# A pre-norm attention block and GeGLU network on one core: residual rows preset in PSUM, a seventh joint pair of F tiles, more turning by DMA, last heads passed on in halves

## The chip, the cores and the metric

The kernel runs on one core of a Trainium2 chip. The metric is device time of one execution in microseconds (us): the median of three runs of the kernel before is 639.09 us (638.98 to 639.78). A measurement of this kernel can tell a change from none from about 0.2% on. The core has TensorE (PE, matrix products into PSUM), VectorE (DVE), ScalarE (ACT), GpSimd (POOL), which sees SBUF only, and SyncE (SP), which issues every DMA here.

## The reference

All in float32, S = 2048 tokens, D = 512, H = 32 heads of 16, window of 8 keys with step 2, F = 1792:

```
qkv = layernorm(x) @ wqkv                       # D -> 3 D
logits[s, w] = q[s] . k[s - 2 w] / 4, w = 0..7  # per head, masked where s - 2 w < 0
o = softmax(logits) @ v[s - 2 w]
h = x + o @ wo
n = layernorm(h)
out = h + (gelu(n @ w_gate) * (n @ w_up)) @ w_down
```

## The kernel before, in words

**Tiling.** The tokens are cut into four chunks c = 0..3 of 512 (rows j = 0..3 of 128). Chunks 0 and 2 hold the even tokens, 1 and 3 the odd ones, so that the step of 2 falls away. Every product is done three times with operands split into a high and a low part (hi x hi, hi x lo, lo x hi), so a 512-wide contraction for 512 columns takes 12 matmuls of 128x512. `split` makes the parts: a cast on ACT and a subtraction on DVE or POOL.

**Projections.** For chunks 1 to 3 q and k of two row tiles are computed together by `project_pair`, with 7 block products of 6 matmuls (42) where the plain way takes 48; the sums that this scheme needs are made by `sums` (of x) and `weight_sums`. `prep` takes x already transposed from DRAM (`xt`) and subtracts the mean, which `stats` computes and PE spreads over the partitions with four transposes.

**Attention(c).** For four groups b of 8 heads, `logits` (products and sums on DVE), `softmax` and `values` (a product on DVE, a tree of additions `pv` on DVE or POOL). The output `o` is transposed, either by PE (`transpose4`, read from PSUM) or by a DMA (`crossed`: an ACT copy that separates the 16-bit halves, a transposing DMA, an ACT copy that joins them, then `split` from SBUF). `CROSS_O` lists the groups b for which the DMA does it; for chunk 0 there were none.

**Tail(c).** `wo` products for the four row tiles (12 matmuls each) into a PSUM bank, `aux` for chunks 1 and 2. DVE adds the residual rows (L775) into `h`, `norm` follows on DVE and POOL, then a transpose to hT, by DMA for chunks 1 and 2 (`CROSS_H`).

**FFN(c).** For each of the 14 F tiles f: a gate and an up product (12 matmuls each), gelu on ACT, a product on DVE, `split_g`, and two steps later (`flush`) the down product, 12 matmuls into the four banks `acc`. `finish` adds h to each bank on DVE (L875) and sends the rows out.

**The last two chunks (`last_two`).** F tiles are taken in pairs for chunks 2 and 3 together (`joint`), 7 block products of 6 matmuls for gate and 7 for up, that is 84 where two chunks and two tiles take 96. The first F tile of `EARLY` pairs is run for chunk 2 alone before (`early_step`), with its first half kept for the joint part. With `PAIRS = 6` two F tiles were left that both chunks did by themselves: chunk 2 ahead of the joint part, chunk 3 behind it. The gate-times-up results for chunk 3 are kept and their down products come last (`rest`).

**Order.** Every operation goes into a list with its engine, a duration and its dependencies. `schedule` runs the list as in time, by rank, and so fixes the order on each engine; `SHIFTS` are nudges to the ranks of stretches of the list, `SWAPS` move single operations between DVE and POOL. On the chip each engine works through its own instructions strictly in that order.

Of the kernel before, what the change touches and what calls it, by code (L numbers as in the profile page):

```python
# [16 lines left out]
P = 128  # L17
D = 512
# [20 lines left out]
FROM, TO = 52, 18  # L39
# [5 lines left out]
PAIRS = 6  # L45
EARLY = 2
# [192 lines left out]
def tile_block(ctx: ExitStack, tc: tile.TileContext, x: bass.AP, xt: bass.AP, wqkv: bass.AP, wo: bass.AP,  # L239
# [248 lines left out]
    def prep(c, j):  # L488
# [10 lines left out]
        if j % 2:  # L499
            sums(c, j // 2, xcs[j - 1], xc)  # L500
# [703 lines left out]
```

## Time and profile before

| | |
|---|---|
| median of three runs | 639.09 us |
| the profiled execution's own time | 640.41 us |
| its span, first to last instruction | 638.5 us |
| PE busy | 628.6 us (98%), 2816 matmuls and transposes |
| DVE, ACT, POOL busy | 497.4, 372.4, 386.9 us |
| DMA | 133.50 MB, mean 209 GB/s |
| granted TensorE clock | 0.999 |

A matmul's busy time is its own duration, and successive ones overlap, so a busy share of 98% tells where PE stood still but not how much work it had. The work is read from the start times: in a run of matmuls without waits one starts about every 0.227 us.

### The profile page before, as it was taken

Reading aid. Unit: us, or ns where it says so; the run is one execution under the profiler, and the core shown is the slowest. Engines: PE = TensorE matmul, PEld = TensorE weight load, DVE = VectorE, ACT = ScalarE, POOL = GpSimd, SP = SyncE. Lnnn points to the kernel's source line nnn. Section 1 sums busy time; section 2 is a strip of 40 time slices with the busy share of each in tenths; the row PEclk is TensorE's granted clock in tenths of the full one; section 3 lists DMA queues with packets and bytes.
Section 4 is the critical chain, followed back from the end, with each engine's and each line's share of the span. In section 5 each row is a group of like instructions: output and inputs, shape, how many; then the busy total and the mean of one; then the engine's idle time right before and its main releaser. Section 6 shows DMA issues by size and latency. Waiting matters only on the chain. (4 is left out here: it accounts for less than half of the span.)

```text
span 638.5 us, 8214 instructions
## 1 busy us (share of the span) xinstructions
PE 628.6 (98%) x2816; PEld 517.4 (81%) x2816; DVE 497.4 (78%) x548; ACT 372.4 (58%) x632; POOL 386.9 (61%) x350
## 2 busy tenths in 40 slices
PE   8999999999999999999999999999999999999997
PEld 8887788887888887877888788888888888888886
DVE  5879989999999999999989999978665633535322
ACT  6796444455554765776786579847455554533341
POOL 3598998943898798477647675628466876400000
PEclk9999999999999999999999999999999999999999
DMA  8759656497859969989997689960432123214362
GB/s 303 247 208 309 239 202 234 152 368 264 285 174 313 289 225 288 305 239 329 357 326 252 230 183 249 274 231 16 149 117 99 59 74 132 83 50 146 82 193 91
DMA packets 66857, 133.50 MB, mean 209 GB/s; under 512 B 24816, under 2 KB 24816, under 8 KB 66304
## 3 DMA queue, kind: packets, MB, share of 16 engines
q1 hardware_dynamic: 66816, 132.99, 63.7%
q8 instruction: 22, 0.36, 0.2%
q14 instruction: 19, 0.16, 0.1%
HBM read 101.19 MB, written 26.80 MB: 200 GB/s over the span
## 5 line engine op out<-in xcount | busy, mean ns | idle before, releaser
L740 POOL TENSOR_TENSOR pv<-pv 128x1024 f32<-128x1024 f32 (+1 forms) x51 | 99.6, 1964 | 20.6 <-DVE pv L735 19.8
L810 PE MATMUL acc<-dnh,gh 128*128 128x512 f32 x224 | 87.2, 390 | 0.0
L812 PE MATMUL acc<-dnh,gl 128*128 128x512 f32 x224 | 87.2, 389 | 0.0
L811 PE MATMUL acc<-dnl,gh 128*128 128x512 f32 x224 | 87.1, 389 | 0.0
L691 DVE TENSOR_TENSOR pk<-kw,qp 128x2048 f32<-128x2048 f32 x32 | 72.9, 2278 | 5.9 <-ACT qp L684 4.4
L735 DVE TENSOR_TENSOR pv<-vw,qp 128x2048 f32<-128x2048 f32 x32 | 72.4, 2279 | 1.7 <-ACT qp L684 0.5
L694 DVE TENSOR_REDUCE lg<-pk 128x128 f32<-128x2048 f32 x32 | 72.6, 2273 | 0.2
L399 PE MATMUL pg<-hTh,gu 128*128 128x512 f32 x256 | 68.9, 391 | 2.1 <-POOL gu L327 0.8
L399 PE MATMUL pu<-hTh,gu 128*128 128x512 f32 x256 | 68.7, 390 | 0.7 <-POOL gu L327 0.7
L399 PEld LDWEIGHTS pg<-hTh,gu 128*128 128x128 f32 x256 | 47.7, 188 | 13.3 <-ACT hTh L326 1.4
L399 PEld LDWEIGHTS pu<-hTh,gu 128*128 128x128 f32 x256 | 47.9, 188 | 11.0 <-POOL gu L327 1.2
L812 PEld LDWEIGHTS acc<-dnh,gl 128*128 128x128 f32 x224 | 42.0, 188 | 8.8
L810 PEld LDWEIGHTS acc<-dnh,gh 128*128 128x128 f32 x224 | 42.0, 188 | 8.8
L811 PEld LDWEIGHTS acc<-dnl,gh 128*128 128x128 f32 x224 | 42.0, 188 | 8.7
L327 POOL TENSOR_TENSOR gl<-g,gh 128x512 fp32r<-128x512 f32 x25 | 33.1, 1325 | 19.2 <-ACT gh L326 19.0
L327 POOL TENSOR_TENSOR gu<-fraw,gu 128x512 fp32r<-128x512 f32 x23 | 30.1, 1323 | 23.9 <-ACT gu L326 23.9
L326 ACT CAST gh<-g 128x512 fp32r<-128x512 f32 x44 | 27.2, 619 | 21.9 <-DVE g L867 12.0
L825 ACT CAST dnh<-fraw 128x512 fp32r<-128x512 f32 x40 | 24.6, 619 | 25.9 <-PE acc L812 17.3
L399 PE MATMUL pg<-hTl,gu 128*128 128x512 f32 x128 | 34.5, 391 | 0.4 <-DVE hTl L327 0.2
L399 PE MATMUL pu<-hTl,gu 128*128 128x512 f32 x128 | 34.2, 389 | 0.0
L1014 ACT COPY jt<-pa 128x512 f32<-128x512 f32 x32 | 18.8, 588 | 24.3 <-PE pa L982 20.0
L867 DVE TENSOR_TENSOR g<-pu,g 128x512 f32<-128x512 f32 x32 | 21.9, 684 | 11.3 <-PE pu L399 10.1
(290 smaller groups left out, 1509.3 us busy)
## 6 DMA issues: line engine op xcount, KB each, us to landing
fraw<-in_wffn_dram SPq DMA_DIRECT2D x46, 768.0 KB, 5.8
kw<-kv SPq DMA_DIRECT2D x16, 704.0 KB, 5.7
vw<-kv SPq DMA_DIRECT2D x16, 704.0 KB, 5.9
dnl<-ld SPq DMA_DIRECT2D x40, 256.0 KB, 3.0
gu<-ld SPq DMA_DIRECT2D x18, 512.0 KB, 4.5
kv<-qkvt SPq DMA_DIRECT2D x32, 256.0 KB, 2.6
ld<-gu SPq DMA_DIRECT2D x14, 512.0 KB, 4.4
x<-in_x_dram SPq DMA_DIRECT2D x16, 256.0 KB, 5.4
```

Of the source, the lines that this page charges most:

```text
L326: act(490 if psum_src else 525, lambda: nc.scalar.copy(hi(), src()), r, [wh])
L327: sub = lambda eng: eng.tensor_tensor(lo(), src(), hi().bitcast(F32), op=ALU.subtract)
L399: nc.tensor.matmul(acc(), a, b, start=(p == k == 0), stop=(p == n - 1 and k == KD - 1))
L691: nc.vector.tensor_tensor(pr(), k4, q2.unsqueeze(2).to_broadcast([P, 2, W, QF]), op=ALU.mult)
L694: dve(2195, lambda pr=pr, jj=jj: nc.vector.tensor_reduce(lg()[:, i, jj:jj + 2], pr().rearrange("p j w (h d) -> p j w h d", d=DH), axis=AX. ...
L735: nc.vector.tensor_tensor(pr().rearrange("p j w (h d) -> p j w h d", d=DH), v5, e5, op=ALU.mult)
L740: either(home, 256 * m, lambda eng, pr=pr, m=m: eng.tensor_tensor(pr()[:, :, 0:m], pr()[:, :, 0:m], pr()[:, :, m:2 * m], op=ALU.add), [], ...
L810: nc.tensor.matmul(a, gh()[:, sl], dh(), start=(i == 0), stop=False)
L811: nc.tensor.matmul(a, gh()[:, sl], dl(), start=False, stop=False)
L812: nc.tensor.matmul(a, gl()[:, sl], dh(), start=False, stop=(i == NF - 1))
L825: act(525, lambda: nc.scalar.copy(dh(), fr()[:, 2]), [(fr, None)], [(dh, None)])
L867: dve(605, lambda: nc.vector.tensor_tensor(g(), ps[1](), g(), op=ALU.mult), [(ps[1], None)], [(g, None)])
```

## The change

What it does, in parts:

1. **Preset PSUM.** `start(c)` copies the rows of h into the four `acc` banks, and the down products then all add to them (`start=False`); `finish` only copies a bank out (`evict`, on ACT, or on DVE by `SWAPS`). In `tail`, ten of the sixteen `wo` banks (`SEEDED`) are filled by ACT with the residual rows before the product; then the bank is copied to h on ACT and `bn_stats` reads the bank itself.
2. **Seventh pair** (`PAIRS` 6 to 7, `EARLY` 2 to 3): no F tile is left for a chunk alone. Chunk 2's down products of the early steps are all issued ahead of tail(3) (`DRAIN`); the ring for intermediate results in the joint part has 5 slots where it had 7 (`JT`).
3. **Turning by DMA** also for o of chunk 0, groups 0 to 2 (`CROSS_O`), and for x of chunk 3 (`CROSS_X`): the rows loaded for the statistics are centred by ACT, turned and split; `xt` is not read for it, and PE does not spread the mean.
4. **Halves.** The last group's o goes on in two parts of two row tiles (`HALVE`), and a `wo` product needs only its own part. Chunk 3's wo goes through three banks (`LASTB`), its residual rows into buffers of their own.
5. **Plain projection** of q and k for the first pair of chunk 1 (`PLAIN`): 48 matmuls, no `sums`.
6. The last row tile of the last chunk leaves PSUM in two halves, by ACT and DVE, with a DMA each; the order of the `qk` banks, the pace of attention (`TO` 18 to 22) and the tables `SHIFTS` and `SWAPS` are new.

```diff
-PAIRS = 6
-EARLY = 2
+PAIRS = 7
+EARLY = 3
-CROSS_O = ((), (0, 1, 2, 3), (0, 1, 2, 3), (0, 1, 2))
+CROSS_X = (3,)
+PLAIN = ((1, 0),)
+SEEDED = [(1, j) for j in (1, 2, 3)] + [(2, j) for j in range(4)] + [(3, j) for j in (1, 2, 3)]
+LASTB = ("qp", "mm0", "mm1", "qp")
+JT = ("q0", "q1", "o1", "lg", "ex")
+HALVE = (0, 1, 2, 3)
+CROSS_O = ((0, 1, 2), (0, 1, 2, 3), (0, 1, 2, 3), (0, 1, 2))
 SHIFTS = (
-    (232, 45, "PE", -8320), (1524, 9, "ACT", 7257), (1661, 68, "DVE POOL", 2376), (810, 7, "DVE", 146), (1093, 5, "DVE POOL", -8370),
+    (102, 130, "PE DVE ACT POOL SP", 1338), (1243, 51, "DVE POOL", 516), (1684, 47, "PE", 2945), (439, 11, "PE", -678), (1244, 116, "POOL", 483),
...
+    def evict(dst, src, r, w, home="ACT"):
+        ns = {"ACT": 490, "DVE": 605}
+        o = plan.add(home, ns[home], lambda: nc.scalar.copy(dst(), src()) if o.engine == "ACT" else nc.vector.tensor_copy(dst(), src()), r, w)
...
         if c in CROSS_X:
+            act(700, lambda: nc.scalar.activation(t(), t(), AF.Identity, bias=mv()[:, j, 0:1]), [(mv, j)], [(t, None)])
+            turn([(t, None)], t, xc)
...
+            if seeded:
+                act(490, lambda acc=acc, j=j: nc.scalar.copy(acc(), rows[j][0]()), rows[j][1], [(acc, None)])
             mm(acc, [...], "wo",
-               [[(oh, None), (wo_h, None)], [(oh, None), (wo_l, None)], [(ol, None), (wo_h, None)]])
-            dve(605, lambda hj=hj, acc=acc: nc.vector.tensor_tensor(hj(), acc(), hj(), op=ALU.add), [(acc, None), (h, None)], [(h, j)])
+               [rh + [(wo_h, None)], rh + [(wo_l, None)], rl + [(wo_h, None)]], seeded=seeded)
+            if seeded:
+                evict(hj, acc, [(acc, None)], [(h, j)])
+                xh = norm(hj, [(h, j)], f"h{c}_{j}", "ACT" if c in ONACT else "DVE", acc, [(acc, None)])
...
-            dve(605, lambda j=j: nc.vector.tensor_tensor(h()[:, j], accs[c][j](), h()[:, j], op=ALU.add),
-                [(accs[c][j], None)], [(h, j)])
+                evict(lambda j=j: h()[:, j], accs[c][j], [(accs[c][j], None)], [(h, j)], "DVE" if c == NC - 1 and j % 2 else "ACT")
     def start(c):
+        for j in range(J if SEED else 0):
+            evict(accs[c][j], lambda j=j: hres[c]()[:, j], [(hres[c], j)], [(accs[c][j], None)])
...
+        if DRAIN:
+            flush(c, 0)
         tail(d)
```

The tables also move instructions. Three places matter below. In the rows, the first name is what is written, then what is read; the last two numbers before the buffer's own are chunk and row (or F) tile, and what stands in brackets is the engine or DMA queue waited for.

On PE, at the end of chunk 2's FFN, the kernel before goes on like this (acc are the down products, pg and pu the gate and up products of chunk 3's own F tiles):

```order
L812 MATMUL acc_2_3_4180<-dnh_2_13_5134,gl_2_13_5326 128x512
L399 MATMUL pg_3_1_5362<-hTh_3_4034,gu_3_1_5142 128x512 x4
L399 MATMUL pg_3_1_5362<-hTl_3_4050,gu_3_1_5142 128x512 x4
...
L399 MATMUL pu_3_0_5421<-hTl_3_4050,gu_3_0_5288 128x512 x4
L399 MATMUL pu_3_0_5421<-hTh_3_4034,gu_3_0_5288 128x512 x4
L810 MATMUL acc_3_0_5436<-dnh_3_1_5222,gh_3_1_5413 128x512 [waits Activation_49]
```

and the changed kernel like this:

```order
L906 MATMUL acc_2_3_3916<-dnh_2_13_5254,gl_2_13_5441 128x512
L904 MATMUL acc_3_0_5476<-dnh_3_0_5340,gh_3_0_5419 128x512 [waits DVE_49]
L905 MATMUL acc_3_0_5476<-dnl_3_0_5338,gh_3_0_5419 128x512 [waits DMAHW3_49]
...
L904 MATMUL acc_3_1_5482<-dnh_3_0_5340,gh_3_0_5419 128x512 [waits Activation_49]
...
L904 MATMUL acc_3_2_5495<-dnh_3_0_5340,gh_3_0_5419 128x512 [waits Activation_49]
...
L904 MATMUL acc_3_3_5498<-dnh_3_0_5340,gh_3_0_5419 128x512 [waits Activation_49]
```

The 48 gate and up matmuls between the two chunks' down products are gone, and each bank's first down product of chunk 3 waits for the engine that presets it.

On ACT, at the same place, the changed kernel has these rows (h_2 from acc_2 is the copy out, acc_3 from h_3 the preset; rows 0 of the presets and 2 of the copies are on DVE):

```order
L349 CAST gh_3_1_5457<-gs_v1_4353 128x512 [waits PE_49,Activation_49]
L919 CAST dnh_3_2_5464<-fraw_3_2_5342 128x512 [waits DMAHW4_49,PE_49]
L308 COPY h_2_2828<-acc_2_0_3877 128x512 [waits PE_49]
L308 COPY h_2_2828<-acc_2_1_3927 128x512 [waits PE_49]
L308 COPY acc_3_1_5482<-h_3_4049 128x512 [waits Activation_49]
L308 COPY h_2_2828<-acc_2_3_3916 128x512 [waits PE_49]
L308 COPY acc_3_2_5495<-h_3_4049 128x512 [waits DVE_49]
L308 COPY acc_3_3_5498<-h_3_4049 128x512 [waits Activation_49]
```

None of these copies was there before; ACT had only casts at this place.

On ACT, in the tail of chunk 1, the changed kernel has these rows (wo_1 from h_1 is the preset, h_1 from wo_1 the copy out, a_o the copies around a transposing DMA):

```order
L860 COPY wo_1_1_2419<-h_1_1333 128x512 [waits DVE_49]
L349 CAST gh_0_11_2427<-g_0_11_2380 128x512 [waits DVE_49]
L377 COPY a_o_1_3_2_2396<-o_1_3_2283 128x2x256 [waits DMAHW1_49,Activation_49]
L349 CAST oTh_1_2024<-a_o_1_3_2_2396 128x256 [waits Activation_49]
L308 COPY h_1_1333<-wo_1_1_2419 128x512 [waits PE_49]
L860 COPY wo_1_2_2466<-h_1_1333 128x512 [waits DVE_49]
```

The copy out and the next preset stand behind a copy that waits for a transposing DMA; before, the bank was freed by one addition on DVE.

## Rows read from the trace of the kernel before

**Rows 1.** Stretches: length, busy of each engine (instructions), granted clock, DMA share, GB/s.

```profile
150.00:200.00 50.00, 49.79 (x221) 40.62 (x220) 47.50 (x39) 27.73 (x48) 38.82 (x28) 1.00 0.75 254
200.00:250.00 50.00, 48.48 (x213) 39.48 (x213) 49.46 (x41) 30.68 (x48) 43.10 (x33) 1.00 0.83 261
250.00:300.00 50.00, 48.49 (x212) 39.18 (x211) 45.41 (x51) 33.52 (x51) 30.66 (x28) 1.00 0.95 296
500.00:550.00 50.00, 50.00 (x222) 41.41 (x221) 21.46 (x27) 27.08 (x47) 37.13 (x40) 1.00 0.23 79
620.00:638.50 18.50, 14.58 (x65) 11.74 (x63) 4.97 (x8) 2.91 (x5) 0.00 (x0) 0.96 0.30 103
```

**Rows 2.** Chain that ended last: start, us from there to the next, what.

```profile
408.81 2.72 PE pg L399 x12
418.78 0.44 PE tp_o L338 x4
```

**Rows 3.** Waits of PE: who for whom, us in total, times, longest.

```profile
PE pg L399 <- POOL gu L327: 0.8, 1, 0.8
PE pg L399 <- ACT hTh L326: 0.8, 1, 0.8
PE pu L399 <- POOL gu L327: 0.7, 1, 0.7
PE pg L399 <- ACT g L861: 0.6, 1, 0.6
PE wo L399 <- DVE h L775: 0.5, 1, 0.5
```

**Rows 4.** Groups on DVE: busy, mean ns of one, idle before, releasers.

```profile
L775 DVE TENSOR_TENSOR h<-wo,h 128x512 f32<-128x512 f32 x16 | 11.0, 686 | 3.9 <-PE wo L399 3.8
L875 DVE TENSOR_TENSOR h<-acc,h 128x512 f32<-128x512 f32 x16 | 10.7, 687 | 7.0 <-PE acc L812 7.0
L602 DVE SCALAR_TENSOR_TENSOR qkvt<-qkb,mvx,qkvt 128x512 f32<-128x512 f32 x6 | 4.5, 743 | 1.5 <-PE qkb L585 1.5
L327 DVE TENSOR_TENSOR oTl<-tp_o,oTh 128x512 fp32r<-128x512 f32 x5 | 3.4, 686 | 1.0 <-ACT oTh L326 1.0
L327 DVE TENSOR_TENSOR oTl<-a_o,oTh 128x512 fp32r<-128x512 f32 x3 | 4.4, 1471 | 0.0
L327 DVE TENSOR_TENSOR hTl<-a_h,hTh 128x512 fp32r<-128x512 f32 x4 | 3.4, 856 | 0.5 <-ACT hTh L326 0.5
L740 DVE TENSOR_TENSOR pv<-pv 128x1024 f32<-128x1024 f32 x6 | 9.5, 1588 | 0.0
L740 DVE TENSOR_TENSOR pv<-pv 128x512 f32<-128x512 f32 x7 | 6.5, 930 | 0.1
L742 DVE TENSOR_TENSOR o<-pv 128x256 f32<-128x256 f32 x13 | 10.2, 794 | 0.0
```

**Rows 5.** Groups on ACT, columns as in rows 4.

```profile
L1014 ACT COPY jt<-pa 128x512 f32<-128x512 f32 x32 | 18.8, 588 | 24.3 <-PE pa L982 20.0 <-DVE pa L1020 4.3
L326 ACT CAST gh<-g 128x512 fp32r<-128x512 f32 x44 | 27.2, 619 | 21.9 <-DVE g L867 12.0 <-DVE g L1011 8.8 <-DVE g L1082 1.0
L350 ACT COPY a_o<-o 128x1024 uint16<-128x1024 uint16 x11 | 11.5, 1042 | 1.3 <-DVE o L742 1.1 <-DVE hTl L327 0.2
L354 ACT COPY a_o<-o 128x1024 uint16<-128x1024 uint16 x11 | 15.0, 1368 | 1.2 <-DMA o<-a_o 1.2
```

**Rows 6.** DMA issues: queue, form, count, KB each, median us to landing.

```profile
qd<-qkvt SPq DMA_DIRECT2D x12, 256.0 KB, 2.6
o<-a_o SPq DMA_TRANSPOSE x11, 4.3
```

**Rows 7.** Waits of ACT between 50 and 430 us, columns as in rows 3.

```profile
ACT dnh L825 <- DMA fraw<-in_wffn_dram: 6.1, 2, 4.2
```

**Rows 8.** Last instructions of PE and DVE in order of time: start, us, what.

```profile
633.51 0.39 PE L812 MATMUL acc<-dnh,gl 128*128 128x512 f32 x1
632.58 2.73 DVE L875 TENSOR_TENSOR h<-acc,h 128x512 f32<-128x512 f32 x4 [5.00 <-PE acc L812]
```

More of the change, by code (lines that the diff above doesn't have):

```diff
@@ L287, in either @@
         return o
+    def evict(dst, src, r, w, home="ACT"):
+        ns = {"ACT": 490, "DVE": 605}
+        away = "DVE" if home == "ACT" else "ACT"
+        o = plan.add(home, ns[home], lambda: nc.scalar.copy(dst(), src()) if o.engine == "ACT" else nc.vector.tensor_copy(dst(), src()), r, w)
+        o.other = away, ns[away]
+        return o
     def dma(dst, src, nbytes, r=(), w=(), eng=None, **k):
@@ L382, in norm, with mm @@
         return dst
-    def mm(acc, triples, nm, reads, chain=(), single=None):
+    def mm(acc, triples, nm, reads, chain=(), single=None, seeded=False):
         n = len(triples)
@@ L498, in prep @@
         xcs[j] = xc
-        if j % 2:
+        if j % 2 and (c, j // 2) not in PLAIN:
             sums(c, j // 2, xcs[j - 1], xc)
@@ L523, in sums @@
         plan.floor = 0
-    wT = {}
+    wT, held = {}, []
     def weight_sums():
@@ L543, in weight_sums, with put @@
             h, l, ph, pl = wT[i]
-            act(950, lambda h=h, src=src: nc.scalar.copy(h(), src()), [r], ph)
-            either("DVE", 1024, lambda eng, h=h, l=l, src=src: eng.tensor_tensor(l(), src(), h().bitcast(F32), op=ALU.subtract), [r] + ph, pl)
+            def put(h=h, l=l, ph=ph, pl=pl, src=src, r=r):
+                act(950, lambda: nc.scalar.copy(h(), src()), [r], ph)
+                either("DVE", 1024, lambda eng: eng.tensor_tensor(l(), src(), h().bitcast(F32), op=ALU.subtract), [r] + ph, pl)
+            if slot or not PLAIN:
+                put()
+            else:
+                held.append(put)
         for i, (s, h) in {0: (1, 0), 1: (1, 1), 6: (0, 1)}.items():
@@ L607, in project_pair @@
         product(0, A, True)
-        scaled(A, 1, j0)
-        product(1, B, True)
-        added(B, 1, j0)
+        if SEEDQK:
+            evict(B, A, [(A, None)], [(B, None)])
+            product(3, C, True)
+            product(1, B, False)
+            scaled(B, 1, j0)
+        else:
+            scaled(A, 1, j0)
+            product(1, B, True)
+            added(B, 1, j0)
         product(4, A, False)
         scaled(A, 0, j0)
-        product(3, C, True)
+        if not SEEDQK:
+            product(3, C, True)
         product(5, A, False)
@@ L1036, in joint @@
                 out_of((1, 1), C, u3, tmp[2 * n + s][-1])
-                if n == s == 0:
+                if n == s == 0 and not DRAIN:
                     flush(c, 0)
@@ L1140, in tile_block @@
             project_pair(c, p)
+            if held and (c, p) == PLAIN[-1]:
+                held.pop()()
         for j in range(J):
```

254 lines of the change are left out of this document (163 added, 91 removed), and 9 rows, old and new, of the table SWAPS.

## The prediction, made before the result was known

> **What bounds the kernel now.** I read the stretches first. PE is busy for 49.79 of 50 us at 150 to 200, for all 50 at 500 to 550, and falls short by 1.52 and 1.51 us in the two stretches from 200 to 300; at the end it has 14.58 of 18.5 [rows 1]. The granted clock is 1.00 in all but the last, so PE is at its upper level and no gain is to be had there. DVE is nearly full in the same front part (47.50, 49.46, 45.41 of 50) and half idle behind (21.46) [rows 1]. So behind about 360 us PE's own work is the time, and before that PE and DVE are close rivals. The chain of waits gives the price of PE's work: 12 matmuls of 512 columns in 2.72 us, 0.2267 each, and four transposes in 0.44, 0.11 each [rows 2]. The waits of PE after the start are few: 0.8, 0.8, 0.7, 0.6 and 0.5 us, 3.4 together; they fall at 238 to 288 us and at 359 and end with POOL, ACT and DVE [rows 3].
>
> **The change part by part.** The order of instructions gives the counts.
>
> *PE's work.* The seventh pair takes 84 matmuls where two plain steps took 96: 12 x 0.2267 = 2.72 us off. The plain projection of one pair adds 6: +1.36. Three groups of o of chunk 0 leave PE (12 transposes of 0.11, -1.32), and so does the spreading of chunk 3's mean (4, -0.44). Sum -3.12. All of it stands in PE's own queue, so it counts in full wherever PE is not waiting.
>
> *DVE up to the end of attention(3).* Of the additions of the residual to wo (686 ns), seven go in chunks 1 and 2 and one DVE copy, taken at the same price, comes: -4.1 us. Of the eight additions to acc (687 ns) in chunks 0 and 1 three stay as copies: -3.4. The plain pair drops three combined scalings (743 ns): -2.2. Chunk 0 drops four low parts of o from PSUM (686 ns) and gets two halves, which no row shows; I put one at 0.42, between half of 686 ns and all of it: -1.9. Four low parts of hT pass to POOL (856 ns): -3.4. Against that, `SWAPS` gives DVE four tree additions of 1024 (1588 ns) and five of 512 (930 ns) and takes six of the last step (794 ns): +6.4 + 4.7 - 4.8 = +6.3. Sum -8.7 [rows 4]. What it is worth is only the waits of PE which a lighter DVE, and a POOL relieved of those trees, can end: of the 3.4 us at most all, at least nothing. They ended with three engines, and one of these (ACT) gets heavier, so I take half: -1.7.
>
> Here a row speaks against the change: a low part of o read from PSUM takes DVE 686 ns, one read from SBUF after a DMA took 1471 [rows 4]. The Trainium skill (SBUF — State Buffer, Who interferes with whom) has the reason: a DVE instruction with two SBUF inputs waits while GpSimd reads SBUF, one with a single SBUF input does not. If all three turned groups of chunk 0 met POOL that way, DVE would have 3 x 0.785 = 2.4 us more, the relief would be 6.3 in place of 8.7, and my half would shrink to -1.2. The order puts most such low parts on POOL, so I keep -1.7.
>
> *Presets of the wo banks.* No row shows a copy from SBUF to PSUM. The nearest are ACT's copy out of PSUM, 588 ns, and its cast within SBUF, 619 [rows 5]; I take 0.6 for each preset and copy out, and the two are so close that the range does not need both. In chunk 1 the bank `aux` was freed by one DVE addition; now it needs a copy out (0.6, with `bn_stats` beside it on DVE) and the preset (0.6), some 1.5 us with the steps between them. Between the second wo product and the third the order leaves PE ten matmuls of other tiles, 2.27 us; between the third and fourth eight, 1.81. So the preset is hidden if ACT is free, with 0.3 to 0.8 to spare, and each microsecond that ACT is held longer is a microsecond of PE. Queued behind the waiting wo product on PE are FFN matmuls which nothing else delays. In chunk 2 eight lie between the first two products and thirty or more behind; chunk 3 has three banks. I take +0.5 for all ten, bounds 0 and +7 (see the slower rival).
>
> *Presets of acc.* For chunks 0 to 2 they come into banks that stand free before the first down product, behind several gate and up products, and cost nothing; without that cover it would be 0.7 per chunk. Between chunks 2 and 3 the cover is gone: the 48 gate and up matmuls that stood there are now joint work. From the end of the last product on acc_2_0 PE needs acc_3_0 after 3 x 0.68 = 2.04 us, and then one more bank every 0.68. ACT has first the cast of a g whose slot frees only one down product earlier, and a cast of down weights, so its first copy out starts about 0.6 late and ends at 1.2; DVE presets bank 0 by 2.0; ACT then copies bank 1, presets it by 2.45 (wanted at 2.72), copies bank 3 by 3.05 and presets bank 2 by 3.75, wanted at 3.40, and bank 3 by 4.3, in time. A stall of 0.35 with 0.6 per copy: +0.4, bounds 0 and +2 (the cast of weights waits for a DMA).
>
> *The last rows.* The last product on acc_3_2 starts at 633.51, three more follow, so PE ends at 633.51 + 3 x 0.227 + 0.39 = 634.58; DVE's four chained additions end at 632.58 + 2.73 = 635.31 [rows 8]. Two engines that share the four rows, with the last one halved, end about 0.45 behind PE, at 635.05. The transfers behind keep their length: -0.2, bounds -0.4 and +0.3 (two transfers of shorter rows).
>
> *ACT and the DMAs.* ACT gets 9 copies out of wo banks, 10 of acc and 25 presets, 44 x 0.6 = 26 us, and seven turned tiles at 1.04 + 1.37 [rows 5], 17 us; with 28 to 34 of 50 busy in the front [rows 1] there is room, but not at every moment. A turned tile lands after 4.3 us, a plain transfer of 256 KB after 2.6 [rows 6]; both turned groups lie early, far ahead of their readers, and cost nothing. Without that cover it would be the 4.3.
>
> *Sum.* -3.1 - 1.7 + 0.5 + 0.4 - 0.2 = -4.1 us, against the profiled execution: 640.4 to 636.3. The median lies 1.3 below that execution, so the prediction is 639.09 - 4.1 = **635.0 us**. With no waits ended it would be 636.7; the forecast's own range is 633 to 637.5.
>
> **The rivals.**
>
> *All waits go.* DVE was the true limit up to 360 us; 8.7 us less of it ends all 3.4 us of waits, and presets and hand-over are free: -3.1 - 3.4 - 0.2 = -6.7, 632.4 us. For it: DVE at 49.46 of 50 in the stretch with the most waits. Against: only 0.5 of the 3.4 names DVE.
>
> *Presets in part late.* The presets of chunks 1 and 2 and the hand-over cost 2.5 together and no wait ends: -3.3 + 2.5, 638.3 us, not to be told from before.
>
> *Slower: ACT's queue.* In chunk 1's tail the copy out and the next preset stand behind a copy that waits for a transposing DMA. Two instructions (1.2 us) lie between the DMA's start and that wait, so ACT can stand 4.3 - 1.2 = 3.1 us; with 1.5 behind it that is 4.6, and PE's cover is 2.27: 2.3 late, three times in chunk 1, 7 us. That such waits hold ACT is shown by one of 4.2 us for the weights of a down product [rows 7]. Time: 639.09 - 3.1 - 0.2 + 0.4 + 7 = 643.2 us. It decides from 4.2 us of late presets on. Against: the turned rows were issued before the wo product that precedes, whose 2.72 us count as cover too.
>
> The Trainium skill (Advanced Engine Details and Errata, X-Bar Transpose (TRN2)) has it that transposing DMAs are as fast as plain ones. Then ACT would stand 1.7 less, each preset would be 0.6 late, and this rival would be 638.0, no slower than before. The rows say 4.3 against 2.6, so I leave it its chance.
>
> **How the numbers follow.** Forecast 0.52, all waits gone 0.16, presets in part late 0.16, slower 0.16. About 0.2% (1.3 us) is what a measurement of this kernel can tell from no change, so faster is below 637.8 and slower above 640.4: faster 0.68, same 0.16, slower 0.16. The range goes down to 631.8, a little below the case of all waits gone, and up to 640.5, which leaves out the slower rival and little else.
>
> **What would show it.** In the changed profile 22 fewer PE instructions; PE's waits at 200 to 360 us down to about 1.7; no wait of a wo product for ACT above 0.5; at the hand-over between chunks 2 and 3 a wait of acc for ACT of some 0.4; the last copy ending 0.45 behind PE. If wo or acc products wait for ACT with more than 4 us in all, or if DVE is still full while PE waits as before, the prediction is wrong.

## The result and the profile after

The changed kernel took 642.01 us in the median of seven runs (640.39 to 643.19), the kernel before beside it 639.07 (638.23 to 640.27): a ratio of 1.004 with a 95% interval from 1.0023 to 1.0057. It is slower by 0.4%, and the forecast of 635.0 was wrong in sign. The profiled execution of after lies at the median, 642.01, with a span of 640.2; that of before had 640.41 and 638.5. Three of after's seven runs had a mean granted clock of 0.998 or more and took 640.4 to 640.9 us, the other four had 0.996 or 0.997 and took 642.0 to 643.2; the profiled one is among the four.

The first part of after's page has busy time, share of the span and instructions of each engine:

```profile
span 640.2 us, 8279 instructions
PE 628.1 (98%) x2794; PEld 515.7 (81%) x2794; DVE 487.0 (76%) x525; ACT 413.9 (65%) x706; POOL 387.8 (61%) x360
```

PE has the 22 instructions fewer that were forecast (2816 before), and ACT 41.5 us more work (forecast 43). DVE has 10.4 less over the whole kernel; the 8.7 that were forecast stood for a part of it and are taken up below. What did not come out is where PE stands. Three of the stretches of [rows 1], and two shorter ones:

```profile
150.00:200.00 50.00, 49.18 (x220) 40.49 (x219) 46.67 (x40) 32.13 (x52) 38.60 (x29) 1.00 0.94 314
200.00:250.00 50.00, 50.00 (x222) 41.42 (x221) 45.46 (x40) 31.17 (x51) 47.16 (x37) 1.00 0.78 232
250.00:300.00 50.00, 47.38 (x200) 37.95 (x199) 42.55 (x43) 39.80 (x61) 23.20 (x22) 0.97 0.93 300
400.00:425.00 25.00, 24.45 (x108) 19.56 (x107) 18.59 (x18) 23.28 (x38) 19.24 (x14) 1.00 0.80 236
425.00:450.00 25.00, 22.94 (x108) 17.92 (x106) 20.00 (x43) 16.15 (x37) 17.45 (x25) 1.00 0.24 78
```

From 150 to 200 PE falls short by 0.82 us (before 0.21). From 200 to 250 it is now full, where it fell short by 1.52. From 250 to 300 it falls short by 2.62 (before 1.51), and the clock is down. And from 400 to 450 it falls short by 2.6 us, in a stretch where the kernel before had none:

```profile
400.00:425.00 25.00, 25.00 (x114) 20.68 (x113) 21.64 (x28) 17.67 (x26) 11.73 (x10) 1.00 0.92 296
425.00:450.00 25.00, 25.00 (x119) 20.62 (x118) 21.27 (x45) 14.25 (x33) 15.55 (x23) 1.00 0.07 22
```

PE's waits in after (who for whom, us in total, times, longest) give the places. Of those in [rows 3] the ones for POOL and DVE are gone, and the one of 0.8 for hTh, which was at 281 us, stands at 152 now. These have come or grown:

```profile
PE pg L428 <- ACT g L955: 2.2, 1, 2.2
...
PE tp_h L361 <- DVE mv_h L406: 1.0, 1, 1.0
...
PE tp_h L361 <- DVE xhat_h L409: 0.8, 1, 0.8
PE wo L428 <- ACT wo L860: 0.5, 2, 0.3
PE pg L1182 <- ACT m1s L1187: 0.5, 1, 0.5
PE pa L1090 <- ACT tt L1024: 0.5, 1, 0.5
PE pa L1090 <- ACT jt L1122: 0.3, 1, 0.3
```

**Where it is lost.** I measured PE's lost time as the distance between starts of successive matmuls beyond 0.2267 us (0.11 for transposes). Against before, after gains 0.3 up to 200 us, loses 0.6 net between 200 and 300, gains 0.2 up to 400, loses 4.6 between 400 and 456 and 0.1 behind. That is 4.8 lost against 3.1 of work saved, and the difference is the 1.6 by which PE's last matmul ends later in the profiled execution (634.58 before, 636.21 after). Of the 4.6, 1.2 are lost ahead of the first row of tail(3), 3.1 from its second row (row 1) to the first joint product (pa) and 0.4 behind it. Pa itself starts at 449.12 before and 450.20 after. From there to the end the work of both is equal, and after takes 0.6 longer (190.0 us against 189.4). The medians differ by 2.9, which is 1.3 more than the profiled executions: before's lies that much above its median, and no trace shows why.

**First place, 283 us.** This is chunk 0's `finish`, chunk 1's `start`, and attention(2) beside them. The columns are start, length, instruction and idle time before it; first PE, then ACT:

```profile
283.17 1.07 PE L428 MATMUL pu<-hTh,gu 128*128 128x512 f32 x4
286.41 2.07 PE L428 MATMUL pg<-hTh,gu 128*128 128x512 f32 x4 [2.18 <-ACT g L955]
288.29 1.71 PE L428 MATMUL pg<-hTl,gu 128*128 128x512 f32 x4
289.84 1.09 PE L428 MATMUL pg<-hTh,gu 128*128 128x512 f32 x4
```

```profile
279.67 1.63 ACT L308 COPY acc<-h 128x512 f32<-128x512 f32 x3
282.77 1.28 ACT L789 ACT_TABLE_LOAD   x1 [1.47 <-DVE pv L810]
284.06 0.39 ACT L789 ACTIVATE qp<-lg 128x256 f32<-128x256 f32 x1
284.47 1.28 ACT L955 ACT_TABLE_LOAD   x1
285.76 0.60 ACT L955 ACTIVATE g<-pg 128x512 f32<-128x512 f32 x1
```

ACT waits 1.47 us with an exp of attention(2) for a DVE product, then loads two tables (1.28 each), one for the exp and one for the gelu, and only then comes the gelu that frees PE's bank. PE stands for 2.18 us, up to 286.41, and its next two groups of four take 2.07 and 1.71 us instead of 1.07: 1.6 us more, at a lower clock.

**Second place, tail(3).** After's PE between the projection of row 1 and the first joint product:

```profile
428.89 1.17 PE L428 MATMUL wo<-wo_h,oTh 128*128 128x512 f32 x4
...
437.90 0.63 PE L361 MATMUL tp_h<-ident,xhat_h 128*128 128x128 f32 x4 [0.98 <-DVE mv_h L406]
...
447.01 0.63 PE L361 MATMUL tp_h<-ident,xhat_h 128*128 128x128 f32 x4 [0.80 <-DVE xhat_h L409]
...
450.20 1.02 PE L1090 MATMUL pa<-tt,jh 128*128 128x512 f32 x3 [0.48 <-ACT tt L1024]
```

This takes 21.31 us. PE's own work in it is 36 projection matmuls, 36 down products and 16 transposes: 72 x 0.2267 + 16 x 0.11 = 18.1. (The transposes at 437.90 read `xhat_h`, which is done at 437.75; `mv_h` is only what ended last.) In the kernel before, 25.05 us pass from row 1 to pa, and 24.9 of them are work:

```profile
424.07 1.07 PE L399 MATMUL wo<-wo_h,oTh 128*128 128x512 f32 x4
...
449.12 1.07 PE L982 MATMUL pa<-tt,jh 128*128 128x512 f32 x4
```

Between its rows stand 42 early gate and up matmuls of chunk 2 (L1074) and 24 down products. After's 36 down products are those of its three early steps, which `DRAIN` puts ahead of tail(3) in the list; on PE they stand between the rows all the same. There is a third early step in after, but all of its gate and up matmuls lie ahead of row 1, because they use the banks `mm0` and `mm1` which `LASTB` gives to rows 1 and 2. The rows' own chain (projection, copy, `bn_stats`, POOL's root, `xhat`, transpose, hT and the sums for the joint products) now has less PE work beside it than it takes.

### The profile page after: what moved, and what is told of

Its sections match the earlier page's. It is cut to its first block, busy times and chain, and to the rows that moved or that the text cites. A ratio compares the mean times of both kernels' runs of the same rounds, so it can differ in the third digit from the quotient of the medians.

```text
span 640.2 us, 8279 instructions
## 1 busy us (share of the span) xinstructions
PE 628.1 (98%) x2794; PEld 515.7 (81%) x2794; DVE 487.0 (76%) x525; ACT 413.9 (65%) x706; POOL 387.8 (61%) x360
## 4 chain that ended last, share of the span: by engine, by line
PE 74%; DVE 11%; ACT 4%; POOL 4%; issue 4%; DMA 1%; ACTq 0%; POOLq 0%; DVEq 0%
PE pa L1090 10%; PE qkv L428 10%; PE pg L428 7%; PE pu L428 6%; PE pc L1090 6%; PE acc L904 5%; PE acc L906 5%; PE acc L905 5%; PE qka L653 4%; PE wo L428 4%; DVE pk L766 3%; PE qkc L653 2%; DVE pv L810 2%; DVE lg L769 2%; PE qkv L421 2%
## 5 line engine op out<-in xcount | busy, mean ns | idle before, releaser
L815 POOL TENSOR_TENSOR pv<-pv 128x1024 f32<-128x1024 f32 (+1 forms) x42 | 83.7, 1998 | 21.8 <-DVE pv L810 18.9
L428 PE MATMUL pg<-hTh,gu 128*128 128x512 f32 x224 | 61.0, 395 | 3.0 <-ACT g L955 2.2
L428 PE MATMUL pu<-hTh,gu 128*128 128x512 f32 x224 | 59.9, 389 | 0.0
L428 PEld LDWEIGHTS pg<-hTh,gu 128*128 128x128 f32 x224 | 42.4, 190 | 12.5 <-ACT g L955 2.6
L428 PEld LDWEIGHTS pu<-hTh,gu 128*128 128x128 f32 x224 | 42.0, 188 | 8.8
L1122 ACT COPY jt<-pa 128x512 f32<-128x512 f32 x36 | 21.1, 587 | 27.7 <-PE pa L1090 21.7
L1076 POOL TENSOR_TENSOR jl<-fraw,jh 128x256 fp32r<-128x256 f32 (+1 forms) x20 | 19.4, 974 | 23.3 <-PE pa L1090 11.9
L919 ACT CAST dnh<-fraw 128x512 fp32r<-128x512 f32 x42 | 25.9, 618 | 9.9 <-PE acc L906 7.4
L1090 PE MATMUL pa<-tt,jh 128*128 128x512 f32 x112 | 30.3, 392 | 0.8 <-ACT tt L1024 0.5
L428 PE MATMUL pg<-hTl,gu 128*128 128x512 f32 x112 | 30.7, 397 | 0.2 <-POOL hTl L350 0.2
```

The source lines that it names most:

```text
L428: nc.tensor.matmul(acc(), a, b, start=(p == k == 0 and not seeded), stop=(p == n - 1 and k == KD - 1), skip_group_check=seeded)
L815: either(home, 256 * m, lambda eng, pr=pr, m=m: eng.tensor_tensor(pr()[:, :, 0:m], pr()[:, :, 0:m], pr()[:, :, m:2 * m], op=ALU.add), [], ...
L1090: nc.tensor.matmul(acc(), a[:, k], b(k), start=first and p == k == 0, stop=p == 2 and k == 1, skip_group_check=not first)
```

## The experiments

In the code, `(n, m)` in `MOVES` puts operation n of the list just ahead of m, in its engine's queue. The loop that does it stands in the first diff and is the same in all that follow.

**1. The exp behind the gelu.** Theory A: the wait at 283 us is the exp that stands ahead of the gelu on ACT. Rival: the presets and copies of acc hold ACT.

```diff
+MOVES = ((1302, 1303),)
-        for o in plan.schedule():
+        order = plan.schedule()
+        for n, at in MOVES:
+            order.remove(plan.ops[n])
+            order.insert(order.index(plan.ops[at]), plan.ops[n])
...
+        for o in order:
             o.emit()
```

> The changed kernel with one operation moved: on ACT the exp of chunk 2's second group (L789) comes behind the gelu of the first F tile of chunk 1 (L955) instead of ahead of it. Theory A (queue): at 283 us PE waits 2.2 us for that gelu, which stands behind four presets of acc and an exp that waits 1.5 us for a product of DVE (pv, L810); and because PE stood still the granted clock fell to 0.56 to 0.59 from 286 to 290 us, another 1.6 us. Both go: 642.0 - 2.3 - 1.6 = 638.1 us, no wait of PE for g at 283, granted clock 1.00 at 275 to 300. Rival B (the clock falls there whatever PE did): 642.0 - 2.3 = 639.7. Rival C (ACT has too much to do at that place, the wait only moves to DVE's product with g or to the next F tile): 641.5 to 642.5, with a wait of PE of about 2 us for DVE at 284 to 292.

640.54 us (640.15 to 641.15, 9 runs), 1.0021 [1.0011, 1.0030] of before. That lies between the forecasts of rivals B (639.7) and C (641.5 to 642.5); theory A's 638.1 was missed. But the wait is gone and so is the fall of the clock; after and this kernel in the same 25 us:

```profile
275.00:300.00 25.00, 22.65 (x92) 17.98 (x91) 20.98 (x19) 18.97 (x32) 11.84 (x9) 0.93 0.93 335
```

```profile
275.00:300.00 25.00, 24.39 (x105) 19.15 (x104) 23.11 (x22) 18.56 (x33) 12.35 (x9) 1.00 0.98 350
```

At 290 us PE is 3.7 us ahead of after, but at the end only 1.6 (1.5 by the medians): 0.9 is given back up to 297, where an up product waits 0.3 for DVE, and 1.1 at the end of attention(2), where now a wo product waits 0.8 for ACT's cast of o. The waits in tail(3) stay as they were. So what stayed is no more than the 1.6 of the clock, and the wait by itself was worth next to nothing by the end. The runs without a trace fit that: all nine of this kernel have a mean clock of 0.999 or 1.000 and take 640.15 to 641.15, no less than after's three at 0.998 or more. Of the 2.9 us by which after's median is above before's, about 1.5 go with this fall of the clock, and about as much is left without it.

**2. Chunk 1's acc without presets.** The kernel leaves out the four presets, so that h is missing from chunk 1's result.

```diff
+seeds = lambda c: c not in (1,)
-gh()[:, sl], dh(), start=(i == 0 and not SEED), stop=False, skip_group_check=SEED)
+gh()[:, sl], dh(), start=(i == 0 and not seeds(c)), stop=False, skip_group_check=seeds(c))
...
-            evict(accs[c][j], lambda j=j: hres[c]()[:, j], [(hres[c], j)], [(accs[c][j], None)])
+            o = evict(accs[c][j], lambda j=j: hres[c]()[:, j], [(hres[c], j)], [(accs[c][j], None)])
+            if not seeds(c): o.emit = lambda: None
```

> The changed kernel, all orders kept, with the four presets of acc for chunk 1 left out (the output of chunk 1 lacks its residual rows). It takes 4 copies of 0.58, 2.3 us, from ACT between the down products of chunk 0 and the first gelu of chunk 1. Theory A (the exp, not the presets): the exp in the queue still waits until DVE's product pv ends at 282.7 us, so the gelu and PE start as late as before: 642.0, with the wait of PE for g at 283 still at 2.0 to 2.2 us. Rival (the presets are the cost that I had put at nothing): the gelu comes 1.5 to 2.3 us earlier and the clock holds: 638.1 to 640.

642.37 us (1.0055 [1.0042, 1.0067]); the wait for g is still 2.2 us and the clock 0.93:

```profile
275.00:300.00 25.00, 22.68 (x91) 17.90 (x91) 20.90 (x19) 16.83 (x27) 11.84 (x9) 0.93 0.93 334
```

That is theory A: it is the exp's place in ACT's queue, not the presets.

**3. The rows' queue in tail(3).** `bn_stats` ahead of the copy, `xhat` of three rows earlier, the last transpose one product earlier.

```diff
+MOVES = ((1924, 1923), (1952, 1951), (1980, 1979), (1928, 2032), (1956, 1963), (1984, 1988), (2003, 1903))
```

> The changed kernel with seven moves in the tail of chunk 3: the statistics of rows 1 to 3 (bn_stats, L405) come ahead of the copy out of the same bank on ACT, three of DVE's normalised rows (xhat_h, L409) come ahead of work that they stood behind, and the last transpose of hT comes one down product earlier on PE. Theory A: between 435 and 454 us PE waits 1.0 for mv_h, 0.8 for xhat_h, 0.5 for tt and 0.3 for jt because the rows follow each other without other work of PE between, and each row's way through copy, statistics, DVE and POOL is longer than PE's 2.7 us per row; with the shorter way the first two waits go and the others stay: 642.0 - 2.1 = 639.9. If the chain to tt comes earlier too, 639.2. Rival (the waits only move to tt, since the bank of the transposes is one and the combining on DVE is the bound): 641.5 to 642, with a wait for tt of 2 us or more.

641.14 us (1.0034 [1.0023, 1.0045]). The waits for mv_h and xhat_h are gone, and 2.7 us for `tt` stand in their place, as the rival has it; from row 1 to pa it is 21.34 us, where after has 21.31:

```profile
PE tp_h L361 <- ACT tt L1024: 2.7, 2, 1.6
```

The next transposes need the bank from which the previous row is still read: DVE's last read of it ends at 442.85 and at 447.15, and they start 0.14 and 0.15 later (the cast `tt` that is named reads another buffer). The named wait moved, the end did not. The median is 0.9 below after's only because more of its runs kept a mean clock of 0.998 or more; these take 640.5 to 641.3, no less than after's.

**4. Both edits together.**

```diff
+MOVES = ((1302, 1303), (1924, 1923), (1952, 1951), ...)
```

> The two sets of moves together. Theory A: the losses are independent, 642.0 - 3.9 - 2.1 = 636.0 us, faster than the kernel before (639.1) by 3. Rivals: with the clock falling anyway 637.6; if both only move their waits, 641 to 642.

641.09 us (1.0030 [1.0019, 1.0041]), no better than the first alone; the losses are not independent.

**5. More PE work in tail(3).** On top of the first edit, nine matmuls more: three down products are issued twice, which changes chunk 2's result.

```diff
+AGAIN = {1957: 1895, 2003: 1896, 2033: 1897}
...
+            if o.n in AGAIN:
+                plan.ops[AGAIN[o.n]].emit()
```

> The kernel with the gelu first, and three down products of the first early step (acc_2_0 and acc_2_1 and acc_2_2, 3 matmuls each) run once more: ahead of the second and the fourth transpose of hT in the tail of chunk 3 and ahead of the first joint product, the three places at 434 to 448 us where PE waits 1.0, 0.8 and 0.5 us (those products then stand twice in the output of chunk 2). It is 9 matmuls of 0.2267, 2.04 us more of PE's work. Theory A (from the first wo product of chunk 3 to the first joint product the row work on ACT, DVE and POOL sets the time, and PE's saved work ahead of it is worth nothing): they fill the waits, 640.5 to 640.8 us. Rival (PE's work counts in full everywhere, as I predicted): 640.5 + 2.0 = 642.5.

645.10 us (1.0086 [1.0066, 1.0105]), but for another reason: up to pa the 2.04 us more cost 0.1 (448.67, against 448.57 in the first experiment). Then the second group of pa waits 3.6 us for ACT, which stands 4.3 us with a cast of down weights until their DMA lands; the repeated products hold the weight buffers longer. As a whole the run tells nothing; its part up to pa does.

**6. Two edits at the end of attention(3).** Theory: the tail starts too late, since the last o comes late (DVE idles there for 2.3 and three times for some 1.1 us). Four operations of the tree go from POOL to DVE, and row 0 of wo starts earlier; the second kernel moves the rows' operations forward as well.

```diff
+LATER = (1830, 1832, 1835, 1836)
+MOVES = ((1302, 1303), (1834, 1860), (1835, 1860), (1763, 1833), ...)
```

> The kernel with the gelu first, and the end of attention(3) brought forward: four tree additions of the last head group go from POOL to DVE, which sits idle there for 2.3, 1.1, 1.1 and 1.2 us; on ACT the copies for the crossing of o and the copies m1s come ahead of the presets of acc for chunk 2, which PE needs 25 us later; the first wo product of chunk 3 comes ahead of the last early step on PE. Theory A (the wait of wo_3_0 for attention(3), 421.7 us, and what follows it set the time up to the first joint product): wo_3_0 starts at 418.5 to 419.5, the wait for m1s (0.7) goes and the waits of 2.7 us in the tail shrink by half: 640.5 - 0.7 - 1.3 = 638.5 us. Rival (the rows of the tail set the time by themselves, each row 3.7 us through the one bank of the transposes): 639.8.

643.64 us (1.0069 [1.0052, 1.0087]). Row 0 starts at 419.3 (421.66 in the first experiment), but row 1 at 430.25 (427.26) and pa at 451.56: the whole last early step now lies between rows 0 and 1 (half of it in the first experiment), and PE waits there 0.8 for ACT's cast of o and 1.2 for a copy on ACT.

> As the run before, and the rows of the tail moved too: the transposes of row 0 come between the wo products of row 1 and ahead of row 1's statistics, and the statistics and normalised rows of rows 1 to 3 as in the run with the tail of chunk 3 moved. Theory A: row 0's combining is done 3 to 4 us earlier and no longer stands in the way of rows 1 to 3, the waits of the tail are down to 0.5 in all: 640.5 - 0.7 - 2.5 = 637.3 us, below the kernel before. Rival (one bank for all four transposes): 639.5, with waits of tp_h of 2 us.

647.12 us (1.0125 [1.0104, 1.0146]). From row 1 to pa it takes 24.4 us with the same work, with waits of 1.6 to 1.9 for xhat_h, for a preset of acc and for `tt`. The theory is wrong: what the tail gets earlier, other waits take back.

**7. More work again,** with other products, so that no buffer is held longer: six matmuls, 1.36 us.

```diff
+AGAIN = {1957: 1904, 2003: 1905}
```

> The kernel with the gelu first, and two down products of the third early step (acc_2_1 and acc_2_2, 3 matmuls each) run once more, ahead of the second and the fourth transpose of hT in the tail of chunk 3, where PE waits 1.0 and 0.8 us; they keep no weight buffer longer than it is kept anyway (the products stand twice in the output of chunk 2). It is 6 matmuls, 1.36 us more of PE's work. Theory A (from the first wo product of row 1 to the first joint product the row work on ACT, DVE and POOL sets the time): 640.5 to 640.9 us, the first joint product at the same time. Rival (PE's work counts in full): 641.9.

641.14 us (1.0022 [1.0012, 1.0032]; the first experiment 1.0021). The median lies between the forecasts, 0.2 above theory A's 640.9 and 0.8 below the rival's 641.9, so here the trace decides. The wait for mv_h falls from 1.0 to 0.3 and that for xhat_h goes; pa starts at 448.71, 0.14 later:

```profile
427.40 1.17 PE L428 MATMUL wo<-wo_h,oTh 128*128 128x512 f32 x4
...
448.71 1.25 PE L1090 MATMUL pa<-tt,jh 128*128 128x512 f32 x4 [0.49 <-ACT tt L1024]
```

From row 1 to pa 21.31 us again, to the hundredth as in after, in the first experiment (427.26 to 448.57) and in the first kernel of 6 (430.25 to 451.56), with 18.1 us of work there and 19.4 here; in 5 it was 21.34 with 20.1. In this stretch PE's work is not the time.

**8. New orders for both kernels.** Perhaps the tables of the change are only badly fitted, and the kernel before would gain as much from a better order. So both got one: after twice (37 and 35 operations moved, some taken to another engine), before once (13).

```diff
+LATER = (1783, 831, 620, 1226, 1944, 1961, 2000)
+MOVES = ((1939, 1940), (1302, 1383), (546, 858), (1952, 1953), ...)
```

> The changed kernel with the same operations, 37 of them at another place in the list and 7 on the other of two engines. The list is the planner's, which takes it that two engines may read one PSUM bank at the same time and that the exp does not wait for a product pv of the group before; in the built program the second reader of a bank waits for the first (bn_stats for the copy out of wo, 3.4 us of waits of DVE) and the exp waits for pv. The places are chosen with these two waits in the planner's rules. Theory A (the change's saving of PE's work is real and was lost to waits that the planner does not know): PE stands still some 5 us less than the 10.1 us of the changed kernel after 45 us: 637 us, below the kernel before. Rival (the saved work of PE cannot be had since DVE and POOL bound the part up to the first joint product): 640 to 641.

> The same with another choice of places (the gelu first, 35 moves, 9 operations on the other engine). Theory A: 637 us. Rival: 640 to 641.

> The kernel before, ordered anew in the same way (13 moves, 3 operations on the other engine). It has few places where two engines read one bank, so there is less to gain: of its 6.2 us of PE standing still after 45 us about 2 go: 637 to 638 us. Theory A: the changed kernel ordered anew is 1 to 3 us below this one, since it has 3.1 us less of PE's work. Rival (the change gives nothing even with a fitting order): this one is as fast or faster.

After in its first new order: 639.51 us (638.51 to 640.36, 12 runs), 1.0004 [0.9992, 1.0015] of before; in its second 640.45 (1.0015 [1.0005, 1.0025]); before in its new order 638.76 (637.52 to 642.70), 0.9995 [0.9977, 1.0013]. Neither of after's orders reaches the 637 of theory A, and the first is 0.8 above before in its own order. An order brings the changed kernel back to even, not below. In tail(3), from 425 to 450 us, PE is busy for 23.30 of 25 us in after's first new order, and for 24.95 in before's.

From row 1 to pa after's first new order takes 20.7 us and its second 19.7, both with the same 18.1 of work:

```profile
428.48 1.17 PE L428 MATMUL wo<-wo_h,oTh 128*128 128x512 f32 x4
...
448.18 1.24 PE L1090 MATMUL pa<-tt,jh 128*128 128x512 f32 x4
```

So the 21.3 belong to the order of the rows' operations in after, and 1.6 of them can be had. The second order loses as much again elsewhere: from 300 to 400 us PE stands still 2.3 there and 0.5 in after.

**9. The cover taken away from the kernel before.** If the rows' chain and the missing cover are the cause, they must show without any part of the change. All instructions stay; only PE's order in tail(3) changes.

```diff
+MOVES = ((1846, 1888), (1845, 1888), (1848, 1888), (1847, 1888), (1849, 1888), (1854, 1888), (1855, 1888), (1856, 1888), (1857, 1888))
```

> The kernel before with the same instructions, all of them: only PE's order in the last chunk's tail is changed. Three blocks of six early gate and up matmuls (L1074; 3 x 1.37 = 4.1 us) and the twelve down products that stand at 437.63 (2.7 us) go ahead of the projection of row 1, which starts at 424.07. From there to the first joint product (449.12) 25.05 us pass in the kernel before; 18.2 us of work are left in that stretch, as in the changed kernel, where it takes 21.3 us. Theory A (in the tail of the last chunk the rows' chain takes some 21 us, and the work that the third early step and the presets took out of it was its cover): row 1 starts about 430.9, the first joint product comes at 430.9 + 21.3 = 452.2 or later (one bank serves all rows here), PE waits 3 us or more between 431 and 453, mostly for xhat_h, tt or h; 642.2 us, slower by 3 us or more. Rival B (the place of this work does not matter; the changed kernel loses there by its heavier ACT queue and its presets, which this kernel has not): the first joint product stays within 0.5 of 449.1, no wait above 0.5, 639.1 us. In between, about 450.5 and 640.5: both have a part.

645.17 us (643.57 to 645.39), 1.0088 [1.0064, 1.0112]. Pa starts 4.87 later than in before; from pa to the end both take 189.4 us.

```profile
430.39 1.07 PE L399 MATMUL wo<-wo_h,oTh 128*128 128x512 f32 x4
...
453.99 1.07 PE L982 MATMUL pa<-tt,jh 128*128 128x512 f32 x4
```

```profile
PE tp_h L338 <- DVE traw L911: 1.4, 1, 1.4
...
PE wo L399 <- DVE h L775: 1.0, 3, 0.5
PE tp_h L338 <- DVE xhat_h L380: 1.0, 1, 1.0
...
PE tp_h L338 <- ACT tt L916: 0.6, 1, 0.6
```

```profile
425.00:450.00 25.00, 21.30 (x96) 16.04 (x95) 16.07 (x34) 11.22 (x27) 12.97 (x21) 1.00 0.07 22
```

The waits for xhat_h and `tt` are there as in after, with the same 18.1 us of work in the stretch; those for `traw` and h are new. It takes 23.6 us here, 2.3 longer than in after; one bank serves all rows here (the waits for h are of that kind), where the change gives them three. So 6.8 us of work taken out of the stretch shorten it by 1.4. Theory A is right, its pa (452.2 or later) early by 1.8.

## Why the prediction was wrong, point by point

**The step that failed** is the sentence on PE's work: "All of it stands in PE's own queue, so it counts in full wherever PE is not waiting." The -3.12 us itself is right: up to pa, PE has 437.06 us of work before and 433.94 after. But the change also moves work: it takes the early matmuls out from between the rows of tail(3). I read that stretch as one where PE does not wait, since before it did not; it did not because 25 us of work stood there. With 18.1 left, the rows' chain of 21.3 sets the time: 3.1 us are lost there that were not lost before, all that the term of -3.12 had saved. Another 1.2 are lost at the end of attention(3), 0.7 of them by the wait for m1s, and 0.4 behind pa. Experiments 5, 7 and 9 show it from both sides: up to 2.0 us of work put in there costs 0.1 up to pa, and 6.8 taken out there give back 1.4. I did not weigh the place of the third early step at all; the new order of PE in that stretch would have shown it.

**DVE's relief.** Up to the first wo product of chunk 3 DVE is busy for 383.5 us, 389.2 before: 5.7 less, where I had 8.7. Part of what I had not listed is the subtraction `xTl` from SBUF, four times on DVE (4.5 us), before twice (1.5). The waits at 239 to 244 and at 360 did end, as forecast. But the -1.7 was not had: a wait of 0.8 came at 152, and ACT's new order put one of 2.2 us at 283, with 1.6 more for the clock in the profiled execution. I had looked at ACT's queue for presets and not for the exp. The first two experiments show its cause; ending it gave 1.5, not 3.8, as 2.0 came back up to 352 us. No term of the sum stood for a fall of the clock: I had put the clock at nothing to gain, and not at something to lose. It is an order of the tables' making, which another order undoes (experiments 1 and 8).

**Presets of wo.** A preset and a copy take 0.59 us each (forecast 0.6), and wo waits 0.5 for them in all, as forecast:

```profile
L860 ACT COPY wo<-h x7: 580/591/628, 244.9 to 373.2; 128x512 f32<-128x512 f32 x7
L308 ACT COPY acc<-h x15: 582/593/619, 142.3 to 599.1; 128x512 f32<-128x512 f32 x15
L308 ACT COPY h<-wo x9: 562/587/602, 249.2 to 440.1; 128x512 f32<-128x512 f32 x9
```

These rows give the shortest, median and longest time in ns. What was wrong is "`bn_stats` beside it": the two never read the bank together. In five of the ten rows DVE sat idle until ACT's copy from the same bank had ended, once until 432.55 behind a copy from 431.93 to 432.52, for 3.4 us together. The Trainium skill (PSUM — Partial Sum Buffer, PSUM bank collisions raise a hardware error) says that two engines may not touch one bank and partition quadrant at the same time, two readers neither. The trace agrees as far as it goes: the second reader waits for the first in the program, and in none of the ten do the reads overlap; what the chip does when they overlap no run here shows. By itself it was not the time: with `bn_stats` first (experiment 3) the end stayed.

**Presets of acc and the hand-over.** No acc product waits for them in chunks 0 to 2, and leaving those of chunk 1 out gained nothing (experiment 2). At the hand-over between chunks 2 and 3 PE does not wait at all; I had 0.4.

**The last rows.** I had two engines sharing the last bank, 0.45 behind PE. They take turns; PE's last matmul ends at 636.21, the last copy at 637.07, 0.86 behind, where before it was 0.72:

```profile
635.82 0.39 PE L906 MATMUL acc<-dnh,gl 128*128 128x512 f32 x1
636.25 0.37 ACT L974 COPY h<-acc 128x256 f32<-128x256 f32 x1
636.65 0.42 DVE L975 COPY h<-acc 128x256 f32<-128x256 f32 x1 [1.07 <-ACT h L974]
```

So -0.2 was +0.1.

**ACT and the DMAs.** I had 26 + 17 = 43 us more for ACT; it was 41.5.

**The rivals.** The slower one gave 643.2, near the result, but by a mechanism that did not come: wo products wait 0.5 for ACT in all, where it had 7. That it had the right size is chance. That ACT's queue can hold PE is right in kind, but it did so at 283 with an exp. All waits go: those for POOL and DVE went, and others came. None of the rivals had the loss in tail(3).

**What stays open.** Which link of the rows' chain sets the 21.3 us is not settled: when `bn_stats` and `xhat` came earlier (experiment 3), the one bank of the transposes took their place, and which of the moves of after's second new order brought it to 19.7 was not tried. The changed kernel with its third early step left between the rows was not tried, as its banks belong to rows 1 and 2; that the -3.12 would then be had is not shown. Why the clock falls in only four of after's seven runs is open too. None of the orders run beats the kernel before by more than its measurement can tell.

## What to carry to other kernels

A stretch in which the bounding engine never waits may be one where its work just covers another chain. Before work there is counted as a saving, measure that chain from its start to its end, and see how much work the new order leaves beside it. And a heavier queue on an engine with room is read from the order at every place where something bound stands in it, not from its busy share.

## What the runs showed of the hardware

After PE's stand of 2.2 us at 283, the granted clock in after was 0.56 and 0.59, near the lower of its two levels, for some 4 us:

```profile
286.00:288.00 2.00, 1.59 (x4) 1.30 (x5) 1.61 (x2) 1.97 (x4) 0.00 (x0) 0.56 1.01 408
288.00:290.00 2.00, 2.00 (x7) 1.57 (x6) 2.00 (x2) 1.98 (x5) 0.22 (x1) 0.59 0.49 192
290.00:292.00 2.00, 2.00 (x10) 1.61 (x10) 2.00 (x2) 1.99 (x3) 2.00 (x2) 1.00 0.83 258
```

So at this place a wait of 2.2 us cost 3.8. In experiment 2, with the same wait, the clock fell as well, and in 5 it was 0.58 and 0.57 from 455 to 459 us, behind the wait of 3.6; in 1, without the wait, it stayed at 1.00. In experiment 9 the waits of 1.0 and 1.4 us left it at 1.00.
